# Cached attention decode with a gated MLP, one core: the first weight load in two pieces, the bias in one, and a row of tiny reads behind the V loads

## The chip, the core and the metric

The kernel runs on one core of one Trainium2 chip. The metric is device time in microseconds (us) of one execution. The profile is of one such execution. Engines are named as the profile names them: PE (matrix), DVE (vector), ACT (scalar), POOL, and SP, which here only waits and issues DMAs; ACTq and SPq are the issuing sides of ACT and SP. Sixteen DMA engines carry all transfers. A "run" below is one contiguous piece of a transfer: one partition's row of it.

## The reference

Two decode steps (batch 2, one token, D = 576) share an input row `x`. Branch A is attention against a cache of 4096 positions for 32 heads of 128; branch B is an MLP with 4608 hidden units; a sigmoid gate mixes them.

```python
g = sigmoid((x * gate_w).sum(-1, keepdims=True))
q = (x @ wq) as 32 heads of 128
p = softmax(q . k_cache * 128**-0.5)          # k_cache, v_cache: (2, 32, 4096, 128) float32
a = (p . v_cache) @ wo                        # wo: (4096, 576)
b = gelu(x @ w1 + b1) @ w2 + b2               # w1: (576, 4608), w2: (4608, 576)
out = g * a + (1 - g) * b
```

Everything is float32. The two caches are 134 MB each; with the weights the kernel reads 308.6 MB, once.

## The kernel before

**Storage.** Three slots, `slots[0]` to `slots[2]`, each of 128 partitions x 64 KB (8.4 MB), take all large loads in turn. One DMA of a whole slot is 128 runs of 64 KB, one per partition.

**Order of loads.** SP issues all large loads in program order, each as soon as the slot is free: `wq` (its first 512 rows into slot 0 as one DMA, key `s0`, the rest into the end of slot 1), `w1` into slots 1 and 2, and then for the 16 groups of four heads K into slots 0 and 1 in turn (`k_load`) and V into slot 2. K of group i+2 waits for DVE to have read K of group i; V of group i+1 waits for the semaphore `avd`, which PE raises when it has read V of group i. After the last V come `w2` and `wo`, the last rows of `wo` in small pieces. ACT issues `x`, `gate_w`, `b1` and `b2` at the start.

**b1.** The bias of 4608 values lies in `b1T` as 128 partitions x 36 values (144 bytes each). Before, it comes in 16 DMAs of 15, 14, ... 1 and 8 partitions, which share one semaphore. The first of them touches 15 partitions, the next 14 and so on. DVE reads `b1T` once, in the addition at L311.

**Compute.** PE makes q from slot 0 (L245, `q_whole`) and the MLP's first product (L286, L295), after a small product that needs `b2` (L271, `bias2`). DVE multiplies K by q in place (L357) and sums (L359); ACT takes exponentials (L369); PE multiplies by V in a loop (L388, L393, L395); ACT copies the result (L377, L381). At the end DVE and PE form the two output products (L454, L489, L534) and SP and ACT each store a part.

**Waits.** `Order.op` and `Order.dma` (whose DMA issues all carry line L84) put semaphore waits before an instruction from what it reads and writes. V loads behind the first are issued directly at L424, and wait for `avd`.

Of the kernel before, what the change touches and what calls it, by code (L numbers as in the profile page):

```python
# [8 lines left out]
PE = mybir.EngineType.PE  # L9
P = 128  # L10


class Order:
# [50 lines left out]
    def op(self, e, f, r=(), w=(), extra=(), sig=None):  # L64

        self.wait(e, self.deps(r, w) + list(extra))
        ins = f(self.eng[e])
        if sig is not None:
            ins.then_inc(sig, 1)
            return None  # L70
        self.count[e] += 1
        ins.then_inc(self.sem[e], 1)
        t = self.token(e, self.sem[e], self.count[e])
        self.note(t, r, w)
        return t

    def dma(self, e, out, in_, r=(), w=(), extra=(), sem=None, val=16):
        self.wait(e, self.deps(r, w) + list(extra))
        if sem is None and self.spare:
            sem, val = self.spare.pop(0)  # L80
        elif sem is None:
            sem = self.tc.alloc_semaphore(f"d{self.nd}")
            self.nd += 1
        self.eng[e].dma_start(out, in_).then_inc(sem, 16)  # L84
        t = (None, sem, val, dict(self.seen[e]))
        self.note(t, r, w)
        return t
# [11 lines left out]
def body(tc, x, k_cache, v_cache, wq, wo, w1, b1, w2, b2, gate_w, out):  # L99
    nc = tc.nc  # L100
    B, H, SK, DH = k_cache.shape
# [7 lines left out]
    NX = D // P  # L109
    XR = NX * P  # L110
# [3 lines left out]
    FR = F // P  # L114
# [3 lines left out]
    DW = D // 2  # L118
    SCALE = float(DH) ** -0.5
    SLOT = R * DH  # L120
    N1 = NQ - 1

    def sb(name, *shape):
        return nc.alloc_sbuf_tensor(name, list(shape), F32).ap()

    slots = [sb(f"slot{i}", P, SLOT) for i in range(3)]
    bank = [nc.alloc_psum_tensor(f"bank{i}", [P, 512], F32).ap() for i in range(8)]
# [3 lines left out]
    o = Order(tc)  # L131
    op, dma = o.op, o.dma
# [3 lines left out]
    b1T = sb("b1T", P, FR)  # L136
    spare = slots[2][:, 2 * F + 2 * FJ:]
    xg, spare = spare[:B + 1, :D], spare[:, D:]
    b2r, spare = spare[:1, :D], spare[:, D:]
    dma("ACT", xg[:B], x.rearrange("b s d -> (b s) d"), w=["xg"])  # L140
    dma("ACT", xg[B:B + 1], gate_w[None, :], w=["gt_in"])
    b1v, b1sem, at = b1.rearrange("(p r) -> p r", r=FR), tc.alloc_semaphore("b1"), 0
    b1runs = list(range(15, 0, -1)) + [8]
    for i, n in enumerate(b1runs):
        dma("ACT", b1T[at:at + n], b1v[at:at + n], w=[f"b1T{i}"], sem=b1sem, val=16 * len(b1runs))
        at += n
    dma("ACT", b2r, b2[None, :], w=["b2r"])


    hrow1 = w1[:XR].rearrange("(p r) n -> p (r n)", r=NX)  # L150
    wqh = slots[1][:, SLOT - WQ // 2:]
    FA = 3
    dma("SP", slots[0], wq[:XR].rearrange("(p r) n -> p (r n)", r=NX), w=["s0"])
    dma("SP", wqh, wq[XR:].rearrange("q (e n) -> (q e) n", e=2), w=["s1q"])
    dma("SP", slots[1][:, :FA * F], hrow1[:, :FA * F], w=["s1a"])
    dma("SP", slots[2][:, :F], hrow1[:, FA * F:], w=["s2a"])
    w1h = slots[2][:, F:F + F // 2]
    dma("SP", w1h, w1[XR:].rearrange("q (e n) -> (q e) n", e=2), w=["s2h"])
    early = [o.wrote[k][0][1] for k in ("xg", "gt_in", "b2r", "s0", "s1q", "s1a", "s2a", "s2h")]
    hr = slots[2][:, 2 * F:2 * F + FJ]  # L160
    ht = slots[2][:, 2 * F + FJ:2 * F + 2 * FJ]

    def quad(src, i):
        g, b = divmod(i, B)
        return src[b, g * HQ:(g + 1) * HQ].rearrange("h (p r) d -> (h p) (r d)", p=HP)
# [26 lines left out]
    xq = sb("xq", P, NC6, B)  # L192
# [31 lines left out]
    V = "DVE"  # L224
# [35 lines left out]
            ins = q_mm(e, NX + s, wqh, s, True)  # L260
        return ins

    op("PE", q_whole, r=["xq", "s0"], w=["q"])
    op("PE", q_half, r=["xq", "s1q"], w=["q"])


# [36 lines left out]
    for m, k in enumerate(("avp", "cps", "fin")):  # L303
        op("ACT", lambda e, m=m: e.copy(hr[:, m * FC:(m + 1) * FC], hps[m][:, :FC]), r=[k], w=[f"s2r{m}"])  # L304
    hb = sb("hb", P, FR, B)
# [2 lines left out]
    op(V, lambda e: e.transpose(ht.rearrange("p (r i) -> p r i", i=32), hr.rearrange("p (i r) -> p r i", r=FR)),  # L308
       r=["s2r0", "s2r1", "s2r2"], w=["s2t"])
    htv = ht.rearrange("p (r i) -> p r i", i=32)[:, :, :B]  # L310
    op(V, lambda e: e.tensor_add(hb, htv, b1T.unsqueeze(2).to_broadcast([P, FR, B])), r=["s2t"] + [f"b1T{i}" for i in range(len(b1runs))], w=["hb"])  # L311
    op(V, lambda e: e.tensor_mul(gt, hb, hb), r=["hb"], w=["gt"])
    op(V, lambda e: e.tensor_scalar(gt, gt, 0.044715, 1.0, op0=ALU.mult, op1=ALU.add), r=["gt"], w=["gt"])
    op(V, lambda e: e.tensor_mul(gt, gt, hb), r=["gt", "hb"], w=["gt"])
# [24 lines left out]
    def k_load(i):  # L339
        s = i % 2  # L340
        if i == 0:
            free = o.deps([], ["s0"])
            for a, sem in ((0, ksem[0]), (1, k0b)):
                c = slice(a * RH * DH, (a + 1) * RH * DH)
                dma("SP", slots[0][:, c], quad(k_cache, 0)[:, c], w=[f"s0{a}"], extra=free, sem=sem)
            return
        w = ["s0"] if s == 0 else ["s1a", "s1q", "s1"]
        dma("SP", slots[s], quad(k_cache, i), w=w, sem=ksem[s], val=16 * (i // 2 + 1))

    def qk(i):  # L350
        g, b = divmod(i, B)
        s, j = ("s0", 0) if i % 2 == 0 else ("s1", 1)
        k = slots[i % 2].rearrange("p (r d) -> p r d", d=DH)
        q = qps[b][g // 4][:, (g % 4) * DH:(g % 4 + 1) * DH]
        parts = [(0, R, s)] if i else [(0, RH, "s00"), (RH, R, "s01")]
        for lo, hi, key in parts:
            op(V, lambda e, lo=lo, hi=hi: e.tensor_mul(  # L357
                k[:, lo:hi], k[:, lo:hi], q.unsqueeze(1).to_broadcast([P, hi - lo, DH])), r=["q", key], w=[key])
        op(V, lambda e: e.tensor_reduce(stt[j], k, AX.X, ALU.add), r=[s] + [p[2] for p in parts], w=[f"st{j}"])  # L359
        op(V, lambda e: e.tensor_reduce(mxt, stt[j], AX.X, ALU.max), r=[f"st{j}"], w=["mx"])  # L360
        op(V, lambda e: e.transpose(mtt, mxt.to_broadcast([P, 32])), r=["mx"], w=["mt"])
        op(V, lambda e: e.tensor_reduce(nmt[j], mtt, AX.X, ALU.max, negate=True), r=["mt"], w=[f"nm{j}"])  # L362

    def soft(i):
        j = i % 2
        o.wait("ACT", o.deps([f"nm{j}", f"st{j}"], ["pt", "rs"]))
        for h in range(HQ):
            a = slice(HP * h, HP * (h + 1))
            ins = nc.scalar.activation(pt[a, h:R * HQ:HQ], stt[j][a], AF.Exp, bias=nmt[j][a], accum_out=rs[a])  # L369
        ins.then_inc(exps, 1)  # L370

    def gather(i):

        g, b = divmod(i, B)
        j = i % 2
        nc.scalar.wait_ge(avd, i + 1)
        nc.scalar.copy(avs, avp).then_inc(avc, 1)  # L377
        a = slice(32 * (g // 2), 32 * (g // 2) + 32)
        nc.scalar.wait_ge(cmb, i + 1)

        op("ACT", lambda e: e.copy(oS[a, b, g % 2], cps[a, :DH + 1]), r=[f"st{j}", f"nm{j}"], w=[f"oS{i}"])  # L381

    def quad_products(e, v, vin):
        e.wait_ge(exps, 1).then_inc(exps, -1)
        e.wait_ge(vin, 16).then_inc(vin, -16)  # L385
        for t in range(NT):
            j = t % 4
            ins = e.matmul(avp[32 * j:32 * j + 32], pt[:, 16 * t:16 * t + 32], v[:, 512 * t:512 * (t + 1)],  # L388
                           start=(t < 4), stop=(t >= NT - 4))
        ins.then_inc(avd, 1)  # L390
        e.wait_ge(avc, 1).then_inc(avc, -1)  # L391
        for rr in range(4):
            e.matmul(cps[:, :DH], sel[:, rr], avs[:, rr * DH:(rr + 1) * DH],  # L393
                     start=(rr == 0), stop=(rr == 3), skip_group_check=True)
        e.matmul(cps[:, DH:DH + 1], hsel, rs, start=False, stop=True, skip_group_check=True).then_inc(cmb, 1)  # L395


    WA = SLOT // D
    views = {"w2": w2.rearrange("(p r) n -> p (r n)", r=FR), "wo": wo.rearrange("(p r) n -> p (r n)", r=OR)}
    wrow = {}  # L400

    def load_rows(name, lo, hi, s, at, **kw):
        t = slots[s][:, at * D:(at + hi - lo) * D]
        dma("SP", t, views[name][:, lo * D:hi * D], w=[(name, lo)], **kw)
        for r in range(lo, hi):
            wrow[name, r] = t[:, (r - lo) * D:(r - lo + 1) * D], (name, lo)


    k_load(0)
    k_load(1)  # L410
    o.wait("SP", o.deps([], S2 + ["gt_in", "s2r0", "s2r1", "s2r2"]))
    nc.sync.dma_start(slots[2], quad(v_cache, 0)).then_inc(vin, 16)
    for i in range(NQ):
        qk(i)
        if i < NQ - 2:
            k_load(i + 2)
        elif i < N1:
            o.spare = [(sem, 32) for sem in early]
            load_rows("w2", 0, WA, 0, 0, extra=o.deps([], ["s0"]))
        soft(i)  # L420
        if i < N1:
            gather(i)
            nc.sync.wait_ge(avd, i + 1)
            nc.sync.dma_start(slots[2], quad(v_cache, i + 1)).then_inc(vin, 16)  # L424
    o.wait("PE", o.deps(["sel0", "sel1", "sel2", "sel3", "hsel", "pt"], ["avp", "cps"]))
    with nc.Fori(0, NQ, engines=[PE], head_slot={PE: 0}):
        quad_products(nc.tensor, slots[2], vin)
    gather(N1)

# [39 lines left out]
    for gp in range(2):  # L469
# [11 lines left out]
       r=["orr", "rg"], w=["oT"])  # L481
# [57 lines left out]
    last = []  # L539
    for b, e in ((0, "SP"), (1, "ACT")):  # L540
        last.append(dma(e, out[b].rearrange("o (s n) -> (o s) n", n=DO), osb[b::32], r=["osb"]))
    return last


# [26 lines left out]
```

## Time and profile before

| | |
|---|---|
| time, median of 3 executions | 723.52 us (723.47 to 724.15) |
| profiled execution | 723.66 us, its span 721.8 us |
| DVE busy | 598.7 us (83%) |
| PE busy | 220.0 us (30%) |
| ACT busy | 49.6 us (7%) |
| bytes moved by DMA | 308.69 MB in 6912 packets, mean 428 GB/s |

The span runs from the first instruction to the last; the time holds some 1.9 us more. A "packet" in the profile is one run of a transfer, or a 4-byte semaphore write at its end. In answers by stretch of time, the DMA share is the time that the packets which start in the stretch took, over 16 engines' time, so that it can pass 1 in a short stretch; GB/s is the bytes of those packets over the stretch.

### The profile page before, as it was taken

To read this page: it belongs to the slowest core of one execution; us is meant where nothing else is said; L and a number is where in the kernel's file an instruction comes from. 1 tells how busy PE (TensorE), PEld (TensorE's weight loads), DVE (VectorE), ACT (ScalarE), POOL (GpSimd) and SP (SyncE) were. 2 spreads that over 40 slices of the span, in tenths; PEclk is the share of its full clock that TensorE was granted. 3 is DMA by queue.
4 is the path that set the end of the run, shared out by engine and by line. 5 is a ranking of instruction groups with operands and counts; after the bars stand their busy time and mean duration, and the time that the engine had idled before them with its cause. 6 is when DMAs were issued, how large, how long until landed. Compare 5 with 4: busy or idle time off the path is not lost. (4 is left out here: it accounts for less than half of the span.)

```text
span 721.8 us, 4007 instructions
## 1 busy us (share of the span) xinstructions
PE 220.0 (30%) x1720; PEld 78.7 (11%) x1720; DVE 598.7 (83%) x162; ACT 49.6 (7%) x166; POOL 0.7 (0%) x6
## 2 busy tenths in 40 slices
PE   1764005050504132140505060504032140506076
PEld 1221002020101010010102020101001010102022
DVE  2004999999999898989899898989898989899860
ACT  0000010101010101010100001010101010100000
POOL 0000000000000000000000000000000000000000
PEclk9988557575666657575757575666657575757579
DMA  9999999999999999999999999999999999999996
GB/s 407 409 414 456 418 454 418 454 418 451 410 447 425 432 436 421 450 421 450 421 447 425 447 414 447 425 425 443 421 450 421 447 425 447 425 439 425 447 401 273
DMA packets 6912, 308.69 MB, mean 428 GB/s; under 512 B 1004, under 2 KB 1012, under 8 KB 1400
## 3 DMA queue, kind: packets, MB, share of 16 engines
q1 hardware_dynamic: 6632, 308.55, 99.0%
q8 instruction: 5, 0.08, 0.0%
q10 hardware_dynamic: 272, 0.03, 0.0%
q14 instruction: 3, 0.02, 0.0%
HBM read 308.57 MB, written 0.00 MB: 428 GB/s over the span
## 5 line engine op out<-in xcount | busy, mean ns | idle before, releaser
L357 DVE TENSOR_TENSOR slot<-slot,bank 128x16384 f32<-128x16384 f32 (+1 forms) x17 | 275.6, 16214 | 36.4 <-DMA slot<-in_A_k_cache_dram 36.4
L388 PE MATMUL bank<-slot,pt 128*32 128x512 f32 x1024 | 150.3, 753 | 457.1 <-PEq L385 457.1
L359 DVE TENSOR_REDUCE st<-slot 128x128 f32<-128x16384 f32 x16 | 275.5, 17220 | 0.5
L388 PEld LDWEIGHTS bank<-slot,pt 128*32 128x32 f32 x1024 | 41.1, 134 | 553.7 <-issue 553.7
L369 ACT ACTIVATE pt<-st,nm 32x128 f32<-32x128 f32 x64 | 33.0, 515 | 125.0 <-DVE nm L362 120.7
L377 ACT COPY avs<-bank 128x512 f32<-128x512 f32 x16 | 9.4, 586 | 441.0 <-PE bank L388 441.0
L308 DVE STREAM_TRANSPOSE slot<-slot 128x1152 f32<-128x1152 f32 x1 | 2.2, 2202 | 44.9 <-ACT slot L304 44.9
L454 DVE SCALAR_TENSOR_TENSOR slot<-slot,hg 128x576 f32<-128x576 f32 x34 | 24.9, 814 | 0.0
L393 PE MATMUL bank<-avs,sel 128*128 128x128 f32 x128 | 18.1, 284 | 12.7 <-PEq L391 12.7
L245 PE MATMUL bank<-slot,xq 128*32 128x512 f32 x160 | 18.7, 630 | 8.1 <-DMA slot<-in_A_wq_dram 8.1
L393 PEld LDWEIGHTS bank<-avs,sel 128*128 128x128 f32 x128 | 15.5, 191 | 26.8 <-issue 26.8
L369 ACT ACTIVATION_READ_ACCUMULATOR pt<-st,nm 32x1 f32 x64 | 12.5, 195 | 0.0
L286 PE MATMUL bank<-slot,xT 128*32 128x384 f32 x96 | 9.4, 557 | 0.0
L520 DVE COPY pt<-bank 128x288 f32<-128x288 f32 x1 | 0.5, 457 | 10.7 <-PE bank L489 10.7
L489 PE MATMUL bank<-slot,oT 128*2 128x288 f32 x108 | 7.3, 406 | 1.3 <-DMA slot<-in_A_wo_dram 0.8
L180 DVE COPY slot<-slot 3x64 f32<-3x64 f32 x2 | 0.4, 184 | 8.7 <-DMA slot<-in_gate_w_dram 8.6
L245 PEld LDWEIGHTS bank<-slot,xq 128*32 128x32 f32 x160 | 5.0, 117 | 21.0 <-issue 12.8
L381 ACT COPY oS<-bank 32x129 f32<-32x129 f32 x16 | 4.1, 258 | 22.8 <-PE bank L395 22.8
L470 DVE TENSOR_TENSOR avs<-oS,dm 128x256 f32<-128x256 f32 x2 | 0.8, 422 | 5.6 <-ACT oS L381 5.6
L489 PE MATMUL bank<-slot,hg 128*2 128x288 f32 x72 | 5.4, 406 | 0.0
L360 DVE TENSOR_REDUCE mx<-st 128x1 f32<-128x128 f32 x16 | 4.6, 286 | 0.5
L395 PEld LDWEIGHTS bank<-rs,hsel 128*128 128x128 f32 x32 | 4.9, 192 | 0.0
(65 smaller groups left out, 48.1 us busy)
## 6 DMA issues: line engine op xcount, KB each, us to landing
slot<-in_A_k_cache_dram SPq DMA_DIRECT2D x2, 4096.0 KB, 27.5
slot<-in_B_w_dram SPq DMA_DIRECT2D x1, 8064.0 KB
slot<-in_B_w_dram SPq DMA_DIRECT2D x1, 6912.0 KB, 41.3
slot<-in_A_wo_dram SPq DMA_DIRECT2D x1, 5184.0 KB
slot<-in_B_w_dram SPq DMA_DIRECT2D x2, 2304.0 KB, 46.3
slot<-in_A_wo_dram SPq DMA_DIRECT2D x1, 1440.0 KB, 11.6
slot<-in_B_w_dram SPq DMA_DIRECT2D x1, 1152.0 KB, 48.5
slot<-in_A_wo_dram SPq DMA_DIRECT2D x1, 1152.0 KB, 14.0
```

What stands on the lines that cost most here:

```text
L245: ins = e.matmul(qps[b][m][HP * h:HP * (h + 1)], xq[:, c, b:b + 1].to_broadcast([P, HP]), v[:, :, h], start=(c == 0), stop=last, skip_grou ...
L286: ins = e.matmul(hps[m][32 * j:32 * j + 32, :FC], xT[:, c], t[:, at:at + FC], start=(c == 0), stop=False, skip_group_check=True)
L357: op(V, lambda e, lo=lo, hi=hi: e.tensor_mul(k[:, lo:hi], k[:, lo:hi], q.unsqueeze(1).to_broadcast([P, hi - lo, DH])), r=["q", key], w=[key])
L359: op(V, lambda e: e.tensor_reduce(stt[j], k, AX.X, ALU.add), r=[s] + [p[2] for p in parts], w=[f"st{j}"])
L360: op(V, lambda e: e.tensor_reduce(mxt, stt[j], AX.X, ALU.max), r=[f"st{j}"], w=["mx"])
L369: ins = nc.scalar.activation(pt[a, h:R * HQ:HQ], stt[j][a], AF.Exp, bias=nmt[j][a], accum_out=rs[a])
L377: nc.scalar.copy(avs, avp).then_inc(avc, 1)
L388: ins = e.matmul(avp[32 * j:32 * j + 32], pt[:, 16 * t:16 * t + 32], v[:, 512 * t:512 * (t + 1)], start=(t < 4), stop=(t >= NT - 4))
L393: e.matmul(cps[:, :DH], sel[:, rr], avs[:, rr * DH:(rr + 1) * DH], start=(rr == 0), stop=(rr == 3), skip_group_check=True)
L395: e.matmul(cps[:, DH:DH + 1], hsel, rs, start=False, stop=True, skip_group_check=True).then_inc(cmb, 1)
L454: op(V, lambda e: e.scalar_tensor_tensor(wacc[:, b], t, hg[:, r, b:b + 1], wacc[:, b], op0=ALU.mult, op1=ALU.add), r=[key, "hg", f"wacc{b} ...
L489: ins = e.matmul(acc[64 * s + 32 * u:64 * s + 32 * u + B], lhs, t[:, u * DW:(u + 1) * DW], start=False, stop=last, skip_group_check=True)
```

## The change

Three edits. The first DMA of `wq` is cut in two: its first 16 partitions (one run of 64 KB for each of them, key `s0f`), then the other 112 (key `s0`); PE's q product and the first K load wait for both. `b1` comes in one DMA of 128 partitions. Behind each of the 15 V loads in the loop, SP issues one more DMA into a new buffer `probe` of 16 partitions, which nothing reads (NQ is 16, so N1 is 15): n = 1, 2, ... 15 partitions of 8 bytes, taken from `b1`. SP waits for the semaphore `psem` of all of these after it has issued its store.

```diff
+    NE = 16
     N1 = NQ - 1
...
-    b1v, b1sem, at = b1.rearrange("(p r) -> p r", r=FR), tc.alloc_semaphore("b1"), 0
-    b1runs = list(range(15, 0, -1)) + [8]
-    for i, n in enumerate(b1runs):
-        dma("ACT", b1T[at:at + n], b1v[at:at + n], w=[f"b1T{i}"], sem=b1sem, val=16 * len(b1runs))
-        at += n
+    dma("ACT", b1T, b1.rearrange("(p r) -> p r", r=FR), w=["b1T"])
...
-    dma("SP", slots[0], wq[:XR].rearrange("(p r) n -> p (r n)", r=NX), w=["s0"])
+    hrowq = wq[:XR].rearrange("(p r) n -> p (r n)", r=NX)
+    dma("SP", slots[0][:NE], hrowq[:NE], w=["s0f"])
+    dma("SP", slots[0][NE:], hrowq[NE:], w=["s0"])
...
-    op("PE", q_whole, r=["xq", "s0"], w=["q"])
+    op("PE", q_whole, r=["xq", "s0f", "s0"], w=["q"])
...
-            free = o.deps([], ["s0"])
+            free = o.deps([], ["s0f", "s0"])
...
+    probe = sb("probe", NE, 2 * N1)
+    psem = tc.alloc_semaphore("psem")
...
             nc.sync.wait_ge(avd, i + 1)
             nc.sync.dma_start(slots[2], quad(v_cache, i + 1)).then_inc(vin, 16)
+            n = i + 1
+            nc.sync.dma_start(probe[:n, 2 * i:2 * n], b1[:2 * n].rearrange("(p r) -> p r", r=2)).then_inc(psem, 16)
...
     for b, e in ((0, "SP"), (1, "ACT")):
         last.append(dma(e, out[b].rearrange("o (s n) -> (o s) n", n=DO), osb[b::32], r=["osb"]))
+    nc.sync.wait_ge(psem, 16 * N1)
```

On SP at the start of the program, the rows are DMAs with destination, source and shape (partitions x float32 values); minus is before, plus the change:

```order
-L84 DMA slot<-in_A_wq_dram 128x16384
+L84 DMA slot<-in_A_wq_dram 16x16384
+L84 DMA slot<-in_A_wq_dram 112x16384
 L84 DMA slot<-in_A_wq_dram 128x2048
 L84 DMA slot<-in_B_w_dram 128x13824
```

One load has become two, and all later loads of SP stand one place further back.

On SP in the loop over the groups, at its first two rounds:

```order
 L84 DMA slot<-in_A_k_cache_dram 128x16384
-L424 DMA slot<-in_A_v_cache_dram 128x16384
+L427 DMA slot<-in_A_v_cache_dram 128x16384
+L430 DMA probe<-in_B_b_dram 1x2
 L84 DMA slot<-in_A_k_cache_dram 128x16384
-L424 DMA slot<-in_A_v_cache_dram 128x16384
+L427 DMA slot<-in_A_v_cache_dram 128x16384
+L430 DMA probe<-in_B_b_dram 2x2
```

A read into `probe` now stands between each V load and the K load behind it; it waits for nothing of its own.

On ACT at the start, the end of the 16 pieces of `b1` and what follows them:

```order
-L84 DMA b1T<-in_B_b_dram 3x36
-L84 DMA b1T<-in_B_b_dram 2x36
-L84 DMA b1T<-in_B_b_dram 1x36
-L84 DMA b1T<-in_B_b_dram 8x36
+L84 DMA b1T<-in_B_b_dram 128x36
 L84 DMA slot<-in_B_b_dram 1x576
 L208 ACT_TABLE_LOAD
```

Fifteen issues are gone ahead of the load of `b2` (the 1x576) and of ACT's first own instruction.

More of the change, by code (lines that the diff above doesn't have):

```diff
@@ L158, in body @@
     dma("SP", w1h, w1[XR:].rearrange("q (e n) -> (q e) n", e=2), w=["s2h"])
-    early = [o.wrote[k][0][1] for k in ("xg", "gt_in", "b2r", "s0", "s1q", "s1a", "s2a", "s2h")]
+    early = [o.wrote[k][0][1] for k in ("xg", "gt_in", "b1T", "b2r", "s0f", "s0", "s1q", "s1a", "s2a", "s2h")]
     hr = slots[2][:, 2 * F:2 * F + FJ]
@@ L310, in body @@
     htv = ht.rearrange("p (r i) -> p r i", i=32)[:, :, :B]
-    op(V, lambda e: e.tensor_add(hb, htv, b1T.unsqueeze(2).to_broadcast([P, FR, B])), r=["s2t"] + [f"b1T{i}" for i in range(len(b1runs))], w=["hb"])
+    op(V, lambda e: e.tensor_add(hb, htv, b1T.unsqueeze(2).to_broadcast([P, FR, B])), r=["s2t", "b1T"], w=["hb"])
     op(V, lambda e: e.tensor_mul(gt, hb, hb), r=["hb"], w=["gt"])
```

## The prediction, made before the changed kernel had run

> **What bounds the kernel now.** I read the page first: busy shares, the slices, the DMA parts.
>
> ```profile
> span 721.8 us, 4007 instructions
> DVE  2004999999999898989899898989898989899860
> DMA  9999999999999999999999999999999999999996
> DMA packets 6912, 308.69 MB, mean 428 GB/s; under 512 B 1004, under 2 KB 1012, under 8 KB 1400
> q1 hardware_dynamic: 6632, 308.55, 99.0%
> ```
>
> SP's queue (q1) keeps all 16 DMA engines at 99.0% of the span; DVE, the busiest engine, has gaps in many slices. Next, stretches of time (us, busy time of each engine, then granted clock, DMA share, GB/s):
>
> ```profile
> 0.00:22.50 22.50, 3.15 (x16) 2.97 (x16) 4.31 (x25) 1.46 (x2) 0.70 (x6) 1.00 0.91 381
> 22.50:51.50 29.00, 22.38 (x176) 6.74 (x180) 0.00 (x0) 0.00 (x0) 0.00 (x0) 0.91 1.01 433
> 51.50:680.00 628.50, 169.44 (x1226) 59.68 (x1215) 575.00 (x105) 47.26 (x162) 0.00 (x0) 0.63 1.00 434
> 680.00:715.70 35.70, 23.14 (x268) 8.53 (x270) 19.10 (x32) 0.85 (x2) 0.00 (x0) 0.79 0.98 415
> 715.70:717.60 1.90, 1.42 (x40) 0.67 (x32) 0.00 (x0) 0.00 (x0) 0.00 (x0) 1.00 0.21 75
> ```
>
> From 22.5 to 680 us the engines never pause (1.00). So whatever lengthens the stay of a byte on a DMA engine, or leaves an engine idle, adds to the end in full, at any place; whatever happens on PE, ACT or SP counts only if it empties the queue. The waits, and the chain that ended last (start, length, what), agree:
>
> ```profile
> DVE slot L357 <- DMA slot<-in_A_k_cache_dram: 36.4, 11, 3.4
> SPq L84 <- DVE mx L360: 146.4, 16, 36.3
> ...
> 701.24 16.36 DMA slot<-in_A_wo_dram
> ```
>
> DVE waits for K (36.4 us in all), SP waits for free slots with loads still in the queue, and the end hangs on the last pieces of wo.
>
> **How one run goes.** Four short stretches show single runs. The engines' time in one is share x 16 x length; the bytes are GB/s x length.
>
> ```profile
> 1.97:2.45 0.48, 0.00 (x0) 0.00 (x0) 0.00 (x0) 0.00 (x0) 0.00 (x0) 1.00 6.17 2048
> 5.05:5.75 0.70, 0.00 (x0) 0.00 (x0) 0.00 (x0) 0.00 (x0) 0.00 (x0) 1.00 3.46 1498
> 1.87:1.89 0.02, 0.00 (x0) 0.00 (x0) 0.02 (x1) 0.00 (x0) 0.00 (x0) 1.00 0.65 230
> 715.52:715.58 0.06, 0.01 (x2) 0.01 (x4) 0.00 (x0) 0.00 (x0) 0.00 (x0) 1.00 0.59 230
> ```
>
> The first holds 983 KB, 15 runs of 64 KB (the first of wq), in 47.4 us of engine time: 3.16 us each. The second holds the next 16 in 38.8 us: 2.42 us each, or 27.1 GB/s. Sixteen times 27.1 is 433 GB/s, the rate of the whole middle: each engine goes at its own full pace and none is ever slowed by another. The third is x, two runs of 2304 bytes into partitions 0 and 1, side by side on two engines: 0.208 us, 104 ns each. The fourth is six runs of the same size from a load over 128 partitions: 94 ns each.
>
> **The split of wq.** Before, 16 engines write to all 128 partitions, eight each. The trace can't tell whether 27.1 GB/s is the pace of an engine or of the way into the memory that serves eight partitions, because at 128 partitions they come to the same. The split tells them apart: its first piece sends all 16 engines into 16 neighbouring partitions. If the engine is the limit, the piece costs nothing: its runs take 3.16 us, as the first 16 did before. If the ways are, the price depends on how many ways 16 neighbours share: 16 ways, 0; one way, 16 x 2.42 = 38.7 us, 36.3 too many. Between ends so far apart I take the middle by factors, four ways: 4 x 2.42 = 9.7 us, 7.3 too many, for each engine.
>
> [...]
>
> [...]
>
> Then the 112 runs. With ways as the limit, twelve of the sixteen got nothing during the first 9.7 us and still owe eight runs each, 19.3 us: the last is done at 29.0 us where before it was done at 19.3. So +9.7 us is the least that four ways cost, because a way's lost time is never made good while the queue is full. The most: each engine gets seven neighbouring rows, which lie across the borders of ways, and if each run shares its way with another engine throughout, 7 x 2.42 = 16.9 us becomes 33.9: done at 43.5, +24.2 us. Engines out of step soon stop meeting, but the worst of 16 decides. I take the middle by factors, +15.3 us.
>
> **The issue of wq and b1.**
>
> ```profile
> 0.95 0.86 SPq L84 DMA_DIRECT2D slot<-in_A_wq_dram  x2
> 1.79 5.93 ACTq L84 DMA_DIRECT2D b1T<-in_B_b_dram  x16
> 8.05 1.28 ACT L208 ACT_TABLE_LOAD   x1 [8.05 <-issue]
> 14.94 0.17 ACT L208 ACTIVATE gb<-bank 128x2 f32<-128x2 f32 x1 [5.60 <-PE bank L202]
> 23.00 18.73 PE L245 MATMUL bank<-slot,xq 128*32 128x512 f32 x160 [8.11 <-DMA slot<-in_A_wq_dram]
> 47.84 2.25 PE L271 MATMUL bank<-slot 1*128 1x288 f32 x4 [6.11 <-DMA slot<-in_B_b_dram]
> 65.25 0.33 SPq L412 DMA_DIRECT2D slot<-in_A_v_cache_dram  x1
> q10 hardware_dynamic: 19, 0.01, 0.4%
> ```
>
> One more issue on SP, 0.43 us (0.86 for two), delays all later loads by as much; the first 16 runs (2.42 us at least) cover it. Without that cover it is +0.4. In return 16 runs instead of 128 have to be set up before every engine has work: the 15 first runs start over 0.48 us, so at most 0.5 us is gained, and about half of that on average; I put both together at 0.
>
> On ACT 15 issues go, 15/16 of 5.93 = 5.6 us. ACT's next work (8.05 + 1.28) is done at 9.3 us, and ACT then waits 5.6 us for PE: nothing. The load of b2 is issued 5.6 us sooner and its bytes queue behind fewer small ones; PE's wait of 6.11 us at L271 should go. PE then starts the w1 product as soon as w1 is there; the K and V loads behind it (V at 65.25) are issued some 5 us sooner, into a queue that is full (1.00): 0. The next late thing is w1 itself.
>
> The last row is ACT's queue in the first 9 us: 19 packets, 0.004 x 16 x 9.0 = 0.58 us of engine time, 30 ns each with the longer x among them. Before, the engine that is in all of b1's pieces has 16 of these runs; after, eight. That is 0.2 us at most, either way.
>
> **The reads into `probe`.** Fifteen more issues of 0.33 us (as the V load above) on SP. Behind a V load the next K load waits for DVE; the smallest room among the rounds and the last room:
>
> ```profile
> 313.24 0.33 SPq L424 DMA_DIRECT2D slot<-in_A_v_cache_dram  x1
> 318.24 0.33 SPq L84 DMA_DIRECT2D slot<-in_A_k_cache_dram  x1
> ...
> 661.47 0.33 SPq L424 DMA_DIRECT2D slot<-in_A_v_cache_dram  x1
> 666.54 0.33 SPq L84 DMA_DIRECT2D slot<-in_A_wo_dram  x1
> ...
> 699.45 2.23 SPq L84 DMA_DIRECT2D slot<-in_A_wo_dram  x5
> 718.47 0.65 SPq L84 DMA_DIRECT2D out_dram<-pt  x1
> ```
>
> 4.7 us of room against 0.33: no load is late. If that room were gone, the sum would be 5 us on SP and still a full queue. On the engines, 120 runs of 8 bytes and their semaphore writes; the engine in all fifteen gets 30 of them, at 30 ns at most 0.9 us, at least 0. It gave up about 0.2 with b1; I take +0.3. The new wait on `psem` is SP's last act. The fifteenth read follows the V load of 661.47, which PE has read by 699.45 us, when SP is let go for wo; so it is done some 19 us ahead of 718.47 and holds up nothing.
>
> **Code.** SP's program grows by 16 DMAs, ACT's shrinks by 15.
>
> ```profile
> q8 instruction: 5, 0.08, 0.0%
> q14 instruction: 3, 0.02, 0.0%
> ```
>
> A packet of 16 KB (0.08 MB over five) is 0.6 us of one engine at 27.1 GB/s; one more or fewer: 0.6 us either way; I take 0.
>
> **Sum.** The profiled execution took 723.66 us, 0.14 above the median. 723.66 + 15.3 (split) + 0.3 (probe), the rest 0, is 739.3, against the median 739.1.
>
> **Rivals.**
> *The engine is the limit, not the way.* Then wq's runs keep 2.42 us in both pieces, and what remains is +0.3 of probe and at most 0.5 gained at the start: 723.3 to 724, no difference that can be told. [...] It decides where the first 16 runs stay at some 3.2 us.
> *Faster.* The engines end apart: in the last 1.9 us they are at 0.21, worth 0.21 x 1.9 = 0.4 us if evenly spread, so 1.5 us could go, and 0.5 at the start: 721.5. For it: the small reads change who is last. Against: they come to 0.9 us at most on one engine, and the start is one event.
> *Step.* Without the uneven pieces of b1 the engines might keep closer step and meet in the main memory, as the first runs seem to (3.16 against 2.42). If all eight runs of wq went so: 8 x 0.74 = 5.9 us, 729.6. Against: the second runs, still within 0.7 us of each other, already take 2.42.
> *The change doesn't do what it says:* 16 runs might not go to 16 engines but to a few. One engine would need 38.7 us for them: 760. [...]
>
> **Chances.** Ways shared, +9.7 to +24.2: 0.59. Engine the limit: 0.25. Faster: 0.08. Step: 0.04. More than +24.2 (fewer ways than four, or few engines): 0.04. [...] So slower by over 0.2% (1.45 us, about what a measurement of this kernel can tell from no change) 0.67, within it 0.25, faster 0.08. Point 739.1; in its own case 733.2 to 747.7. The range must take in the unchanged case: 722.3 to 746.
>
> **What would show it.** Right: the first stretch below 400 GB/s lasts well past 22.5 us, wq lands past 30 us instead of 23 (PE's first L245 product starts then), the first 16 runs take some 10 us each, everything later is shifted by one amount, and the middle is still at 434 GB/s. PE's wait at L271 is gone in any case. Wrong: PE's L245 starts at 23 us as before; or the middle falls below 430 GB/s, which would put the cost on `probe` or on the step of the engines.

## The result, and the profile after

The changed kernel takes 745.55 us in the median (745.1 to 746.1) against 723.52: a ratio of 1.0303, 95% interval 1.0285 to 1.0321, or 22.0 us more. The profiled execution took 746.1 us, its span 744.2.

From the page after: span, DMA slices, rate in GB/s over 40 slices of 18.6 us, and the DMA parts.

```profile
span 744.2 us, 4010 instructions
DMA  9999999999999999999999999999999999999995
GB/s 170 240 373 407 438 451 426 430 440 444 416 437 441 423 433 440 426 430 447 423 437 437 440 423 437 440 423 433 440 423 433 444 423 430 447 426 433 433 415 239
DMA packets 7056, 308.69 MB, mean 415 GB/s; under 512 B 1148, under 2 KB 1156, under 8 KB 1544
q1 hardware_dynamic: 6888, 308.55, 98.8%
```

The DMA engines are as busy as before (98.8% against 99.0%) with the same bytes, but the first two slices move 170 and 240 GB/s; from about the fifth on the rate is the old one. Engines that show as busy here, then, don't always move bytes at the same pace (a share of 1.07 at 249 GB/s in the second row below, 1.00 at 434 in the last); what the slow stretch hangs on, the experiments show. By stretches (PE, PEld, DVE, ACT and POOL busy, granted clock, DMA share, GB/s):

```profile
1.97:2.85 0.88, 0.00 (x0) 0.00 (x0) 0.00 (x0) 0.29 (x1) 0.00 (x0) 1.00 9.59 1192
9.80:39.30 29.50, 3.15 (x16) 2.98 (x16) 3.54 (x23) 0.17 (x1) 0.00 (x0) 1.00 1.07 249
44.00:75.00 31.00, 29.86 (x280) 10.13 (x284) 0.00 (x0) 0.00 (x0) 0.00 (x0) 1.00 1.02 437
75.00:680.00 605.00, 153.63 (x1096) 54.21 (x1092) 557.77 (x86) 44.31 (x152) 0.00 (x0) 0.62 1.00 434
```

The first row holds the start of the 16 runs of the first piece: 1192 x 0.88 = 1049 KB, and 9.59 x 16 x 0.88 = 135 us of engine time, 8.44 us for a run; the first 15 runs of before took 3.16 each. The second holds the 112: 7.3 MB, 505 us of engine time, 4.5 us a run on average, against 2.42 for the second 16 runs of before. From 44 us on the engines are at 437 and 434 GB/s, as before. Where PE starts its q product, and the small product that waited for b2:

```profile
45.15 19.46 PE L245 MATMUL bank<-slot,xq 128*32 128x512 f32 x160 [28.27 <-DMA slot<-in_A_wq_dram]
64.53 1.23 PE L271 MATMUL bank<-slot 1*128 1x288 f32 x4
```

wq is there at 45.15 us instead of 23.00, 22.15 us later, as much as the whole loss. L271 waits for no DMA any more. A read into `probe` and its neighbours on SP:

```profile
139.63 0.33 SPq L427 DMA_DIRECT2D slot<-in_A_v_cache_dram  x1
140.00 0.34 SPq L430 DMA_DIRECT2D probe<-in_B_b_dram  x1
152.68 0.34 SPq L84 DMA_DIRECT2D slot<-in_A_k_cache_dram  x1
```

It takes 0.34 us, where 0.33 was expected, and the next issue comes 12 us later.

### The profile page after: what moved, and what is told of

The parts are those of the page before. It is cut to its first block, busy times and chain, and to the rows that moved or that the text cites. A ratio compares the mean times of both kernels' runs of the same rounds, so it can differ in the third digit from the quotient of the medians.

```text
span 744.2 us, 4010 instructions
## 1 busy us (share of the span) xinstructions
PE 215.0 (29%) x1720; PEld 78.1 (10%) x1720; DVE 599.0 (80%) x162; ACT 49.5 (7%) x166; POOL 0.7 (0%) x6
## 3 DMA queue, kind: packets, MB, share of 16 engines
q1 hardware_dynamic: 6888, 308.55, 98.8%
## 5 line engine op out<-in xcount | busy, mean ns | idle before, releaser
L388 PE MATMUL bank<-slot,pt 128*32 128x512 f32 x1024 | 146.7, 737 | 466.9 <-PEq L385 466.9
L460 DVE SCALAR_TENSOR_TENSOR slot<-slot,hg 128x576 f32<-128x576 f32 x34 | 24.9, 814 | 0.0
L286 PE MATMUL bank<-slot,xT 128*32 128x384 f32 x96 | 7.9, 487 | 0.0
```

The costliest lines, as they stand in the source:

```text
L286: ins = e.matmul(hps[m][32 * j:32 * j + 32, :FC], xT[:, c], t[:, at:at + FC], start=(c == 0), stop=False, skip_group_check=True)
L460: op(V, lambda e: e.scalar_tensor_tensor(wacc[:, b], t, hg[:, r, b:b + 1], wacc[:, b], op0=ALU.mult, op1=ALU.add), r=[key, "hg", f"wacc{b} ...
```

## The experiments

Each of these differs from the changed kernel unless it says otherwise. Times are medians; the kernel before ran beside them at 723.51 us (first four) and 723.67 us (last four). The last four are one execution each and have no interval; the executions of each of the first three lie within 0.4 us of one another, those of the fourth within 2.6 us.

**The split alone**, in the kernel before:

```diff
-    dma("SP", slots[0], wq[:XR].rearrange("(p r) n -> p (r n)", r=NX), w=["s0"])
+    hrowq = wq[:XR].rearrange("(p r) n -> p (r n)", r=NX)
+    dma("SP", slots[0][:NE], hrowq[:NE], w=["s0f"])
+    dma("SP", slots[0][NE:], hrowq[NE:], w=["s0"])
```

> The kernel before with the split of wq alone (16 and 112 partitions), b1 in 16 pieces, no probe. Theory ways (neighbouring partitions share a way that takes no more than one engine gives): the whole loss is here, wq lands some 20 us later than before, and the time is 743 to 746 us. Rival small reads and step (the probe reads, or the loss of b1's uneven start, slow the engines): 724 us, and wq lands at 23 us.

745.22 us, ratio 1.0299 (1.0283 to 1.0315); PE's q product starts at 45.09 us:

```profile
45.09 18.71 PE L248 MATMUL bank<-slot,xq 128*32 128x512 f32 x160 [28.07 <-DMA slot<-in_A_wq_dram]
67.86 1.81 PE L274 MATMUL bank<-slot 1*128 1x288 f32 x4 [4.06 <-DMA slot<-in_B_b_dram]
```

The split is the whole loss, 21.7 of 22.0 us, with b1 still in its 16 pieces (whose wait for b2 is still in the second row) and no probe.

**All but the split:**

```diff
-    dma("SP", slots[0][:NE], hrowq[:NE], w=["s0f"])
-    dma("SP", slots[0][NE:], hrowq[NE:], w=["s0"])
+    dma("SP", slots[0], hrowq, w=["s0"])
```

> The changed kernel with wq in one DMA again; b1 in one DMA and the 15 probe reads stay. Theory ways: 723 to 724.5 us, no difference that can be told; PE's wait for b2 at L271 is gone and buys nothing. Rival small reads and step: 743 us or more.

724.09 us, ratio 1.0007 (0.9998 to 1.0016): 0.6 us over before, which can't be told from nothing. Its rows of PE and of the first V load:

```profile
23.02 19.24 PE L244 MATMUL bank<-slot,xq 128*32 128x512 f32 x160 [8.06 <-DMA slot<-in_A_wq_dram]
42.20 1.23 PE L270 MATMUL bank<-slot 1*128 1x288 f32 x4
57.58 0.33 SPq L414 DMA_DIRECT2D slot<-in_A_v_cache_dram  x1
```

PE's 6.11 us of waiting for b2 are gone, and SP issues the first V load at 57.58 instead of 65.25 us. The time shows no gain from it: from 51.5 to 680 us the DMA share is 1.00 at 434 GB/s in both kernels, so the load only joins the end of a full queue sooner.

**The cut by columns.** The first piece has as many bytes, but from all partitions:

```diff
-    dma("SP", slots[0][:NE], hrowq[:NE], w=["s0f"])
-    dma("SP", slots[0][NE:], hrowq[NE:], w=["s0"])
+    NC = SLOT // 8
+    dma("SP", slots[0][:, :NC], hrowq[:, :NC], w=["s0f"])
+    dma("SP", slots[0][:, NC:], hrowq[:, NC:], w=["s0"])
```

> The changed kernel with wq cut by columns: a first DMA of 128 partitions x 8 KB (1 MiB, as much as the 16 runs of 64 KB), then 128 partitions x 56 KB. Theory ways: each engine keeps to its own way, so 723 to 724.5 us. Rival cut (any load in two pieces, or a first piece of 1 MiB, costs): 730 to 746 us.

723.83 us, ratio 1.0004 (0.9994 to 1.0013). The first 22.5 us:

```profile
0.00:22.50 22.50, 3.15 (x16) 2.97 (x16) 4.32 (x25) 1.46 (x2) 0.70 (x6) 1.00 0.92 382
```

382 GB/s, where before had 381. Neither a second DMA nor a first piece of 1 MiB costs anything that shows; which partitions a piece covers does.

**The toll twice.** The K load of group 8 is cut in the same way, with two semaphores of its own:

```diff
+        if i == 8:
+            src, free = quad(k_cache, i), o.deps([], ["s0"])
+            dma("SP", slots[0][:NE], src[:NE], w=["s0x"], extra=free, sem=k8a)
+            dma("SP", slots[0][NE:], src[NE:], w=w, sem=k8b)
+            return
```

> The changed kernel with the K load of group 8 cut in 16 and 112 partitions as well. Theory ways: the toll is paid once more, in a place where the queue is full and the engines are out of step: another 18 to 24 us, 763 to 770 us, and DVE waits for that K load some 20 us longer. Rival start (the cost belongs to the first transfers of the program, with cold memory): 746 us.

771.37 us, ratio 1.0666 (1.065 to 1.0682): another 25.8 us. The rate before, during and after that load:

```profile
340.00:357.00 17.00, 0.00 (x0) 0.00 (x0) 14.34 (x1) 1.34 (x6) 0.00 (x0) 0.50 1.02 439
357.00:405.00 48.00, 10.84 (x74) 3.82 (x74) 20.78 (x5) 2.91 (x10) 0.00 (x0) 0.61 1.00 212
405.00:680.00 275.00, 73.37 (x518) 26.06 (x518) 248.20 (x36) 20.35 (x70) 0.00 (x0) 0.63 1.00 434
```

DVE's waits for K (in all, how many, the longest), in the changed kernel and then here:

```profile
DVE slot L357 <- DMA slot<-in_A_k_cache_dram: 42.7, 14, 3.4
DVE slot L365 <- DMA slot<-in_A_k_cache_dram: 68.9, 14, 28.9
```

The rate falls to 212 GB/s for 48 us, which against 434 is 48 x (1 - 212/434) = 24.6 us lost (the profiled execution took 770.42 us, 24.9 more than the changed kernel's median), and one wait of DVE for K is 28.9 us long instead of 3.4 at most. So the toll doesn't need the start of the program; a load cut like this pays it in the middle too. The time is 1.4 us above the upper end of what was expected, and 25.8 us is more than the 22 of the first load; engines that start the piece out of step may be why, which was not tried.

**Which partitions share.** Four kernels cut wq into equal pieces. Halves of 64 neighbouring partitions:

```diff
-    dma("SP", slots[0][:NE], hrowq[:NE], w=["s0f"])
-    dma("SP", slots[0][NE:], hrowq[NE:], w=["s0"])
+    dma("SP", slots[0][:64], hrowq[:64], w=["s0f"])
+    dma("SP", slots[0][64:], hrowq[64:], w=["s0"])
```

> The changed kernel with wq cut in two halves of 64 partitions. [...] Rival odd count (the trouble is the 112, seven rows for each engine): 724 us.

745.21 us, 21.5 more than before. The trouble isn't the odd 112. Eight pieces of 16 partitions, eight apart:

```diff
+    for j in range(8):
+        dma("SP", slots[0][j::8], hrowq[j::8], w=[WQ_KEYS[j]])
```

> The changed kernel with wq in eight DMAs of 16 partitions, the j-th with partitions j, j+8, j+16 and so on, so that the 16 engines write far apart. Ways of eight neighbouring partitions: each engine has a way to itself, 724 us. [...]

745.24 us, 21.6 more than before. Partitions eight apart are still not free of one another. The same with 16 neighbouring rows read, `hrowq[16 * j:16 * j + 16]`:

> Eight DMAs of 16 runs as in the spread kernel, but each reads 16 neighbouring rows of wq and writes every eighth partition. The rows of wq then lie in other partitions than x expects, so the q product is made of mismatched rows; all work is the same. Theory ways: only the partitions written count: the time of the spread kernel. Rival main memory (reads of neighbouring rows collide): as with 16 neighbouring partitions, 9.7 us for each of eight, +58 us, 782 us.

745.47 us. And the reverse, `slots[0][16 * j:16 * j + 16]` written from `hrowq[j::8]`:

> The reverse: each of eight DMAs reads every eighth row of wq and writes 16 neighbouring partitions; the q product is again made of mismatched rows. Theory ways: four ways at a time, 8 x 9.7 = 77 us instead of 19.3: +58 us, 782 us. Rival main memory: the time of the spread kernel.

778.82 us, 55.2 more than before. In two of these kernels, stretches that hold 16 runs each (206 x 5.1 and 112 x 9.4 are both 1.05 MB): first two of eight apart, then two of 16 neighbours.

```profile
12.10:17.20 5.10, 1.15 (x6) 1.06 (x5) 2.55 (x17) 0.17 (x1) 0.00 (x0) 1.00 1.01 206
17.20:22.30 5.10, 0.00 (x0) 0.00 (x0) 0.00 (x0) 0.00 (x0) 0.00 (x0) 1.00 1.00 206
```

```profile
18.50:27.90 9.40, 0.00 (x0) 0.00 (x0) 1.21 (x10) 0.00 (x0) 0.00 (x0) 1.00 1.00 112
27.90:37.30 9.40, 0.00 (x0) 0.00 (x0) 0.00 (x0) 0.00 (x0) 0.00 (x0) 1.00 1.01 112
```

A run takes 5.1 us in the one and 9.4 us in the other, against 2.42 in the uncut load: 2.1 and 3.9 times as long. The halves of 64 neighbours give the same 206 GB/s, 5.1 us a run (12.00 to 17.10 us). So 16 runs at once get here what 7.6 runs, or 4.1, get in the uncut load (206 and 112 GB/s over 27.1); what holds them up, no run shows. The two kernels that differ only in the rows they read (745.24 and 745.47) agree; the two that differ only in the partitions they write (745.24 and 778.82) don't. So the cost hangs on the partitions that are written, and the rows read in main memory have no part in it that shows. The sums fit: 8 x 5.1 - 19.3 = 21.5 us (measured 21.6), 8 x 9.4 - 19.3 = 55.9 (measured 55.2).

## Why the prediction was right, and where its size was off

*The bound.* Right: DMA time at the very start came through to the end in full. What the end shows is 22.0 us, what wq lost is 22.15. That 745.55 us lies inside the range is in part luck: it is 0.45 us below its upper end of 746, and that end was set below the forecast's own upper bound of 747.7.

*The split.* Right that 16 runs into 16 neighbouring partitions slow one another, too small in size: the term was put at +15.3 us, and measured +21.7 with the split alone. That there are ways that serve eight partitions each, that 16 neighbours have four of them, and that an engine takes seven neighbouring rows of the 112 were the author's estimates; no run shows them, and what the runs showed is the time of a run, 8.44 us in the first piece and 4.5 in the second. Its two parts failed in opposite directions. The first piece was put at 7.3 us too many; its runs took 8.44 instead of 3.16 us, 5.3 too many. The 3.16 of before was already 0.74 over the 2.42 of the next 16, and 16 runs into 16 neighbours got a little more than four times the pace of one run in the uncut load (1.05 MB in 9.4 us are 112 GB/s, against 4 x 27.1 = 108). That doesn't explain all of it: where all pieces are 16 neighbours, the first 15 runs took 8.5 us each (a share of 9.09 at 1117 GB/s from 1.97 to 2.85 us) and later ones 9.4, and why the first are shorter stays open. The 112 runs were put at 15.3 - 7.3 = 8.0 us too many; they took 4.5 instead of 2.42 us each, seven times 2.1, 14.6 too many. The step that failed is "engines out of step soon stop meeting", by which a middle value was taken instead of the upper one. The runs grew shorter only for a while, as two stretches of the 112-partition piece show:

```profile
18.00:22.00 4.00, 0.00 (x0) 0.00 (x0) 1.76 (x13) 0.00 (x0) 0.00 (x0) 1.00 0.83 263
34.00:38.00 4.00, 0.00 (x0) 0.00 (x0) 0.00 (x0) 0.00 (x0) 0.00 (x0) 1.00 1.01 230
```

By share and rate, a run that starts in the first of these took 3.3 us, and one in the second 4.6 us again; over the whole piece it was 4.5, near the doubled 4.84. The two parts come to 19.9 us; the other 1.8 of the 21.7 are not accounted for by these means, which leave out how far the last of the 16 engines lies behind the mean. The upper bound of +24.2 us held for this load.

*The pair of x.* It would have been a poor guide to the price. Its two runs of 2.3 KB into partitions 0 and 1 took 104 ns each against 94 for their like, 10% more; the 16 runs of 64 KB into neighbouring partitions took 8.44 us each against 3.16. Why the short ones lost so little, no run shows.

*Issue, b1, b2, probe, `psem`, code.* Right: all of it together, without the split, is +0.6 us, and the interval of its ratio (0.9998 to 1.0016) takes in no change; +0.3 was forecast. PE's wait at L271 went and bought nothing. The issues fitted in their gaps.

*Rivals.* "The engine is the limit" fell with the first runs (8.44 us, where it needed some 3.2). "Step" fell with the kernel without the split and, for the start as a cause, with the toll paid again at group 8. "Few engines" fell too: the 16 runs of the first piece all started between 1.97 and 2.85 us and took 8.44 us each, so 16 were under way at once, where a single engine would have needed 38.7 us for them.

*What would show it.* wq past 30 us, a first stretch far below 400 GB/s, 434 GB/s in the middle and no wait at L271 all came. "Shifted by one amount" came nearly: the issue of the last pieces of wo shifted by 20.4 us (699.45 to 719.87), the end by 22.1. From the chain of waits after:

```profile
719.87 0.33 SPq L84
...
720.72 17.34 DMA slot<-in_A_wo_dram
738.05 0.04 issue
738.10 1.39 PE bank L540 x32
739.49 0.04 issue
739.53 0.70 PE bank L540 x8
```

Here PE waits for the last pieces at 738.05 and 739.49; before, the last DMA ended at 717.60. From the issue of these pieces to that of the store it is 19.0 us before and 20.7 after. In two other kernels with a slowed load this stretch is 19.6 us (the toll twice) and 21.1 (the split alone), so it doesn't follow the size of the loss; the 1.7 us stay open.

## What to carry to other kernels

In a kernel that the DMA engines bound, don't cut a load by partitions: a piece that covers 16, 64 or 112 of 128 partitions ran here at a quarter to a little over half of the full rate (112 GB/s for 16 neighbours, 206 for 64, 249 for 112, against 434), although the DMA share was 1.00 to 1.07. Cut it by columns, which cost nothing that showed in the one cut tried (an eighth and the rest). And read GB/s beside the DMA share: a share of 1.0 at 206 GB/s meant here runs of 5.1 us, not the 2.42 of the uncut load.

## What was not expected of the hardware

The cost isn't quite proportional: a run took 5.1 us in pieces of 16 partitions eight apart, 5% more than twice 2.42, and 9.4 us in pieces of 16 neighbours, 3% less than four times. And runs that had grown shorter didn't stay so: in the 112-partition piece a run took 3.3 us for a while (18 to 22 us) and then 4.6 again (34 to 38 us).
